# Attention into a feed-forward layer on one core: one third tile's scores in another bank pair, the first q scaled on VectorE and loaded in two pieces, four column sums on quarters of the array, and a longer table of order

## The chip, the cores and the metric

The kernel runs on one core of one Trainium2 chip. The metric is device time in microseconds of one execution, the median over the runs. Before the change three runs gave 1102.1, 1102.84 and 1106.57 us, so the median is 1102.84 us.

## What is computed

The reference takes q, k and v of 8 batches, 8 heads, 576 positions and 64 features, and the weights of a feed-forward layer with 512 inputs, 2048 hidden units and 512 outputs:

```python
scores = scale * np.matmul(q, k.transpose(0, 1, 3, 2))
thresh = np.max(scores, axis=-1, keepdims=True) - tau
scores = np.where(scores >= thresh, scores, -1000000000.0)
attn = np.exp(scores - np.max(scores, axis=-1, keepdims=True))
attn = attn / (np.sum(attn, axis=-1, keepdims=True) + 1e-09)
attn_out = np.matmul(attn, v)
x = attn_out.transpose(0, 2, 1, 3).reshape(B * S, H * D)
h = x @ w_in
g = s * np.maximum(h, 0.0) ** 2 + b
out = g @ w_out
```

The term b of g adds to every output the same row: b times the column sums of w_out. The kernel computes that row once ("the sums") and adds it to each finished block.

## The kernel before

**Tiles.** The scores are made in tiles of 128 rows by 576 keys. Batch 0 is done with float32 products by `plain_tile` (36 tiles of four pairs of heads), batches 1 to 7 with pairs of float16 pieces by `split_tile` (252 tiles). A plain tile goes: two matmuls on TensorE write the scores into a pair of PSUM banks (L531), VectorE takes the row maximum (L534), ScalarE the exponent (L538), VectorE drops what is under the threshold and sums (L540), GpSimd and VectorE make the reciprocal (L543, L545), GpSimd scales the row (L546), TensorE transposes it into bank pair `t` (five transposes, L554), ScalarE copies that out (L558), and TensorE multiplies with v into bank `pv` (L567), which ScalarE copies out (L571). The scores of plain tiles lie in turn in bank pair `s` and, in every second tile, in bank pair `o`.

**Weights.** w_in and w_out arrive in float64 (16 pieces each, L651 and L654, 512 KB a piece), are turned into float32 by two operations on ScalarE (L675, L678) and one on VectorE (L670), their sizes are measured with 16 small matmuls for every four pieces (L693, L697), and when all 32 pieces are known a common power of two is found (L703 to L720). Only then ScalarE (L742) and VectorE (L746) split the weights in float16 halves, and only after that the feed-forward layer can start.

**The sums.** `sums(k)` handles four pieces of w_out: four float32 matmuls with a matrix of ones (L773), two after each other on the left 64 columns of the array and two on the right 64, so that two run side by side. Groups 0 and 1 come in the middle of the weights, groups 2 and 3 later (`SUMS_LATE`). VectorE adds each group to a buffer (L779), and one matmul with the constant `both` (L782) adds the two rows that the halves made.

**Feed-forward.** For a block of 256 rows there are 16 steps of 24 matmuls into bank `h` (in the trace line 280, tile h), a chain on ScalarE and GpSimd (L852, L855, L856, L857), and twice six matmuls into bank pair `o` (line 280, tile o).

**The first q.** `Plain.load` issues a pair's q (two transfers of 64 rows by 576), k and v from SyncE. For every pair GpSimd multiplies q by the scale (`scale_q`, L404), once per head, and the scores wait for that.

**Dummies.** 76 matmuls on constants (L988, `keep_busy`) are put where the plan has TensorE free: 16 at the start and 5 for each of the first twelve tiles. Each one runs, wherever it stands.

**The order.** Nothing is ordered by hand: the class `Plan` holds every piece of work with an engine, a cost, its inputs and a due time, places it by list scheduling forwards and backwards, and prints one fixed order for each engine. The table `NUDGES` moves single runs of operations of one engine and cost (kind, first, how many, by how many ns) before the last placing. Each engine then works strictly in this order and waits where an input is late. All loads leave on one queue, SyncE's.

## Time and profile before

| | us |
|---|---|
| three runs | 1102.1, 1102.84, 1106.57 |
| median | 1102.84 |
| the profiled execution, its own time | 1104.32 |
| its span from the first to the last instruction | 1102.5 |
| what lies around the span | 1.82 |
| TensorE busy | 1087.2 |
| ScalarE busy | 962.2 |
| VectorE busy | 913.0 |
| GpSimd busy | 544.4 |

A busy time is the union of an engine's instructions. Matmuls overlap in the pipeline, and their ends are modelled; so the time that a group of matmuls costs is better read from the chain of waits, where a piece reaches from one start to the next.

### The profile page before, as it was taken

The numbers are of one execution on the slowest core, as the hardware profiler recorded it, in microseconds if no ns is written. First come the engines' busy times: TensorE is split into PE (matmuls) and PEld (weight loads), VectorE is DVE, ScalarE is ACT, GpSimd is POOL, SyncE is SP. The second block draws the span as 40 slices with busy tenths as digits, with TensorE's granted clock in tenths as the row PEclk, the third lists the DMA queues.
The fourth block names the chain that finished last, engine by engine and source line by source line (L and its number), as shares of the span: only waits on it lengthen the run. The fifth ranks groups of instructions, "written<-read, shape, count | busy, mean of one in ns | idle before, by whom it ended". The sixth has DMA issues, their size and how long they took to land.

```text
span 1102.5 us, 38419 instructions
## 1 busy us (share of the span) xinstructions
PE 1087.2 (99%) x15026; PEld 927.5 (84%) x15026; DVE 913.0 (83%) x1947; ACT 962.2 (87%) x2293; POOL 544.4 (49%) x1113
## 2 busy tenths in 40 slices
PE   8999999999999999999999999999999999999998
PEld 7876778888888888788888888888888799997886
DVE  6899899999999899999887999988988888884021
ACT  8998998999899999999889998998999899896443
POOL 6646565555555554555444454444646455443200
PEclk9999999999999999999999999999999999999999
DMA  9940279879968988889876789769976987563000
GB/s 269 360 167 1 68 176 182 153 139 168 211 111 164 197 168 160 149 150 172 156 133 113 145 165 180 137 127 191 169 115 130 161 164 132 99 108 60 2 21 21
DMA packets 359078, 157.05 MB, mean 142 GB/s; under 512 B 313328, under 2 KB 340464, under 8 KB 358896
## 3 DMA queue, kind: packets, MB, share of 16 engines
q1 hardware_dynamic: 358896, 154.60, 70.8%
q8 instruction: 118, 1.93, 0.7%
q14 instruction: 64, 0.52, 0.2%
HBM read 46.01 MB, written 9.44 MB: 50 GB/s over the span
## 4 chain that ended last, share of the span: by engine, by line
PE 89%; DVE 3%; DMA 3%; ACT 2%; issue 1%; SPq 1%; POOL 0%; DVEq 0%; ACTq 0%; POOLq 0%
PE o L280 31%; PE h L280 31%; PE pv L631 8%; PE t L280 5%; PE s L280 5%; PE pv L567 2%; PE t L554 2%; PE o L531 1%; PE s L531 1%; DMA eb<-en 1%; DMA ea<-en 1%; DVE em L607 1%; PE h L693 1%; DVE st L599 1%; PE s L594 1%
## 5 line engine op out<-in xcount | busy, mean ns | idle before, releaser
L280 PE MATMUL h<-xp,iw 128*64 128x256 f16 x6912 | 434.8, 273 | 2.4 <-ACT iw L852 2.2
L280 PEld LDWEIGHTS <-iw 128*64 128x64 f16 x6912 | 393.5, 110 | 31.0 <-issue 5.6
L280 PEld LDWEIGHTS <-gs 128*64 128x64 f16 x3456 | 235.8, 110 | 77.9 <-issue 1.0
L857 POOL TENSOR_TENSOR gs<-iw,gs 128x256 f16<-128x256 f32 x272 | 193.2, 711 | 188.4 <-ACT gs L856 77.8
L280 PE MATMUL o<-ow,gs 128*64 128x512 f16 x1944 | 249.6, 379 | 0.0
L616 DVE SCALAR_TENSOR_TENSOR en<-em,st,en 128x576 f16<-128x576 f32 x252 | 207.3, 826 | 21.2 <-ACT en L613 19.4
L613 ACT ACTIVATE en<-em,st 128x576 f16<-128x576 f32 x252 | 193.1, 770 | 12.1 <-DVE st L612 7.5
L280 PE MATMUL o<-iw,gs 128*64 128x512 f16 x1512 | 196.9, 379 | 0.2 <-DVE iw L876 0.2
L601 POOL TENSOR_SCALAR st<-st,wz 128x1 f32<-128x1 f32 x252 | 130.5, 518 | 101.2 <-DVE st L599 66.4
L852 ACT ACTIVATE iw<-h 128x256 f32<-128x256 f32 x288 | 108.6, 377 | 63.3 <-PE h L280 59.5
L610 POOL TENSOR_SCALAR st<-st 128x1 f32<-128x1 f32 x252 | 87.4, 347 | 148.5 <-DVE em L607 95.8
L855 ACT ACTIVATE iw<-iw 128x256 f32<-128x256 f32 x288 | 119.9, 417 | 3.4
L856 ACT CAST gs<-iw 128x256 f16<-128x256 f32 x288 | 116.1, 405 | 7.2 <-PE o L280 3.9
L280 PEld LDWEIGHTS <-ow 128*64 128x64 f16 x1568 | 100.1, 110 | 18.1 <-issue 2.8
L607 DVE SCALAR_TENSOR_TENSOR em<-s,st,em 128x576 f32<-128x576 f32 x126 | 102.2, 811 | 12.8 <-ACT em L605 8.3
L607 DVE SCALAR_TENSOR_TENSOR em<-t,st,em 128x576 f32<-128x576 f32 x126 | 102.2, 811 | 9.6 <-ACT em L605 5.1
L605 ACT ACTIVATE em<-s,st,wz 128x576 f32<-128x576 f32 x126 | 104.0, 825 | 1.1
L605 ACT ACTIVATE em<-t,st,wz 128x576 f32<-128x576 f32 x126 | 103.7, 823 | 0.8 <-DVE vs L464 0.2
L599 DVE TENSOR_REDUCE st<-s 128x1 f32<-128x576 f32 x126 | 94.3, 749 | 9.2 <-PE s L280 6.9
L599 DVE TENSOR_REDUCE st<-t 128x1 f32<-128x576 f32 x126 | 94.4, 749 | 7.3 <-PE t L280 6.1
L603 ACT ACTIVATE st<-st,wz 128x1 f32<-128x1 f32 x252 | 73.1, 290 | 24.4 <-DVE st L599 23.9
L631 PE MATMUL pv<-eb,ow 128*64 128x256 f16 (+1 forms) x588 | 78.9, 286 | 0.3 <-DMA eb<-en 0.3
(188 smaller groups left out, 1606.8 us busy)
## 6 DMA issues: line engine op xcount, KB each, us to landing
ow<-k SPq DMA_DIRECT2D x98, 216.0 KB, 3.8
rk<-in_k_dram SPq DMA_DIRECT2D x29, 288.0 KB, 3.5
iw<-in_moe_w_in_dram SPq DMA_DIRECT2D x16, 512.0 KB, 9.8
ow<-in_moe_w_out_dram SPq DMA_DIRECT2D x16, 512.0 KB, 9.3
out_dram<-iw SPq DMA_DIRECT2D x32, 256.0 KB, 3.5
rq<-in_q_dram SPq DMA_DIRECT2D x28, 288.0 KB, 4.0
rv<-in_v_dram SPq DMA_DIRECT2D x56, 128.0 KB, 3.2
qs<-k SPq DMA_DIRECT2D x14, 216.0 KB, 4.1
```

Of the source, the lines that this page charges most:

```text
L280: nc.tensor.matmul(out[own], stat[:, own], moving, start=start, stop=stop)
L599: dve((667, 750), lambda: nc.vector.tensor_reduce(out=top, in_=ps, axis=mybir.AxisListType.XY, op=ALU.max, negate=True), [bk], [(ks_, 0)], ...
L601: pool((290, 255), lambda: nc.gpsimd.tensor_scalar(out=line, in0=top, scalar1=-1.0, scalar2=va.wz[:, 2:3], op0=ALU.mult, op1=ALU.add), [(k ...
L605: act((716, 885), lambda: nc.scalar.activation(out=halves, in_=ps, func=AF.Exp, bias=bias, scale=va.wz[:, 1:2]), [bk, (ks_, 4), (va.kwz, 1 ...
L607: dve((738, 820), lambda: nc.vector.scalar_tensor_tensor(out=halves, in0=ps, scalar=line, in1=halves, op0=ALU.is_ge, op1=ALU.mult, accum_o ...
L613: act((666, 760), lambda: nc.scalar.activation(out=pieces[:, 0:S], in_=ex, func=AF.Copy, scale=unit), [em_k, (ks_, 3)], [en_k], i)
L616: dve2((728, 830), lambda: nc.vector.scalar_tensor_tensor(out=pieces[:, S + T:2 * S + T], in0=ex, scalar=unit, in1=pieces[:, 0:S], op0=ALU ...
L631: nc.tensor.matmul(ps[j * D:(j + 1) * D], hd.values()[:, (n + 1) % 5, u * D:(u + 1) * D], lazy[("ea", "eb")[j]][:, n, g.c0:g.c0 + g.n], st ...
L852: act((264, 400), lambda: nc.scalar.activation(out=g(), in_=ps, func=AF.Relu, scale=H_DOWN), [h, (f"w{SPARES[(0, 1, 5)[k3]]}", "i", 2)], [ ...
L855: act((307, 430), lambda: nc.scalar.activation(out=g(), in_=g(), func=AF.Square), [kg], [kg], at)
L856: act((295, 405), lambda: nc.scalar.copy(out=hi, in_=g()), [kg], [f"gh{k3}"], at)
L857: do((735, 735) if not self.last else (400, 490), lambda: eng.tensor_tensor(out=lo, in0=g(), in1=hi, op=ALU.subtract), [kg, f"gh{k3}"], [f ...
```

## The change

- The third tile's scores go to bank pair `t`, which the transposes use, in place of `s`.
- For pair 0 both heads' q are scaled by VectorE; the other pairs stay with GpSimd.
- The first head's q of pair 0 comes in two transfers (columns 0 to 127, and the other 448), each scaled by itself; the first tile waits for the small one alone.
- The four matmuls of a group of sums go to four quarters of 32 columns, side by side, with one row of ones for each quarter in `both` (four memsets in place of two).
- The table `NUDGES` keeps its entries, with the kinds renumbered for the new kinds of operation, and grows from 290 to 706 entries.

```diff
 NUDGES = (
-    (65, 55, 78, 6378), (67, 298, 144, 1003), (67, 501, 22, 5345), (38, 97, 63, -9652), (73, 2, 1, -2466), (53, 128, 6, -1430), (20, 46, 18, 3633), (48, 231, 35, -1881),
+    (68, 55, 78, 6378), (70, 298, 144, 1003), (70, 501, 22, 5345), (41, 97, 63, -9652), (76, 2, 1, -2466), (56, 128, 6, -1430), (23, 46, 18, 3633), (51, 231, 35, -1881),
...
+    (58, 203, 1, 3504), (65, 200, 1, 449), (53, 79, 33, -4132), (67, 65, 15, -2135), (59, 177, 50, 1020), (48, 52, 60, -396), (20, 117, 5, 2817), (8, 0, 4, 162),
...
+    Q = P // 4
...
             for j in range(2):
-                dma(144, lambda j=j: nc.sync.dma_start(out=self.get()[1][j * D:(j + 1) * D, j], in_=qT[self.bi, 2 * self.p + j]),
-                    [], [kq + (j,)], at)
+                cut = ((0, P), (P, S)) if not self.p and not j else ((0, S),)
+
+                def part_(c, j=j):
+                    dma(c[1] / 4, lambda: nc.sync.dma_start(out=self.get()[1][j * D:(j + 1) * D, j, c[0]:c[1]],
+                                                            in_=qT[self.bi, 2 * self.p + j, :, c[0]:c[1]]), [], ["q00" if c[1] == P else kq + (j,)], at)
+                part_(cut[0])
                 if not j:
                     dma(295, lambda: nc.sync.dma_start(out=self.get()[0], in_=kT[self.bi, h2].rearrange("h d s -> (h d) s")),
                         [], [kk], at)
+                if len(cut) > 1:
+                    part_(cut[1])
...
-                pool((740, 748), lambda j=j: self.scale_q(j), [k, (self.tag, "z"), "bound"], [k], at)
+                if not self.p and not j:
+                    dve2((150, 230), lambda: self.scale_q(0, 0, P), ["q00", (self.tag, "z"), "bound"], ["q00"], -40)
+                    dve2((460, 540), lambda: self.scale_q(0, P, S), [k, (self.tag, "z"), "bound"], [k], at)
+                elif not self.p:
+                    dve2((560, 640), lambda j=j: self.scale_q(j), [k, (self.tag, "z"), "bound"], [k], at)
+                else:
+                    pool((740, 748), lambda j=j: self.scale_q(j), [k, (self.tag, "z"), "bound"], [k], at)
...
-        def scale_q(self, j):
-
-            q = self.get()[1][:, j]
-            nc.gpsimd.tensor_scalar(out=q, in0=q, scalar1=scale, scalar2=1.0, op0=ALU.mult, op1=ALU.mult)
+        def scale_q(self, j, lo=0, hi=S):
+
+            q = self.get()[1][:, j, lo:hi]
+            (nc.gpsimd if self.p else nc.vector).tensor_scalar(out=q, in0=q, scalar1=scale, scalar2=1.0, op0=ALU.mult, op1=ALU.mult)
...
             for n, f in enumerate(fs):
-                nc.tensor.matmul(bank["h"][n % 2 * D:(n % 2 + 1) * D], ones.bitcast(F32)[:, 0:D], lazy["whole", f, 1],
-                                 start=(n < 2), stop=(n > 1))
-        plan.add("PE", (2 * 870, 2 * 870 + 250), products, [(f"w{f}", "o") for f in fs] + ["ones"], ["h"], at, True)
+                nc.tensor.matmul(bank["h"][n * Q:(n + 1) * Q], ones.bitcast(F32)[:, 0:Q], lazy["whole", f, 1], start=True, stop=True)
+        plan.add("PE", (870 + 120, 870 + 370), products, [(f"w{f}", "o") for f in fs] + ["ones"], ["h"], at, True)
...
-        for j in range(2):
-            nc.gpsimd.memset(both[j * D:j * D + 1], 1.0)
+        for j in range(4):
+            nc.gpsimd.memset(both[j * Q:j * Q + 1], 1.0)
...
-        ti.tag = "o" if i < TWO_BANKS and i % 2 else "s"
+        ti.tag = "t" if i == 2 else "o" if i < TWO_BANKS and i % 2 else "s"
```

The table's rows tell little, so three places of the resulting order are shown. The first is SyncE's queue at the start of the program, where `rq`, `rk` and `xp` are q, k and v of pair 0, `qs`, `en` and `vt` those of pair 1, `k<-in_q` the q of pair 2, and `iw`, `ow` the weights. Before:

```order
L974 DMA tau_t<-in_tau_dram 128x1
L371 DMA rq<-in_q_dram 64x576
L374 DMA rk<-in_k_dram 128x576
L371 DMA rq<-in_q_dram 64x576
L395 DMA xp_129<-in_v_dram 128x2x256
L371 DMA qs<-in_q_dram 64x576
L374 DMA en_77<-in_k_dram 128x576
L395 DMA vt<-in_v_dram 128x2x256
L371 DMA qs<-in_q_dram 64x576
L651 DMA iw_195<-in_moe_w_in_dram 128x4x256
```

With the change:

```order
L1038 DMA tau_t<-in_tau_dram 128x1
L431 DMA rk<-in_k_dram 128x576
L427 DMA qs<-in_q_dram 64x576
L460 DMA xp_131<-in_v_dram 128x2x256
L427 DMA k<-in_q_dram 64x576
L427 DMA rq<-in_q_dram 64x128
L427 DMA qs<-in_q_dram 64x576
L427 DMA rq<-in_q_dram 64x576
L427 DMA rq<-in_q_dram 64x448
L460 DMA vt<-in_v_dram 128x2x256
L431 DMA en_77<-in_k_dram 128x576
L716 DMA iw_200<-in_moe_w_in_dram 128x4x256
```

The first q, the first transfer behind tau before, now stands behind k of pair 0, a q of pair 1, v of pair 0 and a q of pair 2; the first weights move from the tenth to the twelfth place.

The second place is TensorE at the start (`s`, `o`, `t` are the bank pairs, `em` the exponents of a tile, `pv<-qt,ones` the dummies). Before:

```order
L988 MATMUL pv<-qt,ones 128x256 x16
L531 MATMUL s<-rk,rq 128x288 x2
L531 MATMUL o<-rk,rq 128x288 x2
L988 MATMUL pv<-qt,ones 128x256 x10
L531 MATMUL s<-rk,rq 128x288 x2
L531 MATMUL o<-rk,rq 128x288 x2
L988 MATMUL pv<-qt,ones 128x256 x2
L554 MATMUL t<-eb,em_78 128x128 x5
L988 MATMUL pv<-qt,ones 128x256 x8
L554 MATMUL t<-eb,em_79 128x128 x5
L531 MATMUL s<-en_77,qs 128x288 x2
```

With the change:

```order
L1052 MATMUL pv<-qt,ones 128x256 x16
L596 MATMUL s<-rk,rq 128x288 x2
L1052 MATMUL pv<-qt,ones 128x256 x5
L596 MATMUL o<-rk,rq 128x288 x2
L1052 MATMUL pv<-qt,ones 128x256 x5
L596 MATMUL s<-en_77,qs 128x288 x2
L619 MATMUL t<-eb,em_78 128x128 x5
L596 MATMUL o<-rk,rq 128x288 x2
L619 MATMUL t<-eb,em_79 128x128 x5
L596 MATMUL t<-rk,rq 128x288 x2
```

The same 16 dummies stand ahead of the first scores; a tile of pair 1 now comes third, and the tile whose scores lie in `t` comes fifth.

The third place is VectorE at the start. Before:

```order
L1002 TENSOR_SCALAR bound<-bound 128x1
L534 TENSOR_REDUCE st_69<-s 128x1
L534 TENSOR_REDUCE st_70<-o 128x1
L540 SCALAR_TENSOR_TENSOR em_78,st_69<-s,st_69,em_78 128x576
L540 SCALAR_TENSOR_TENSOR em_79,st_70<-o,st_70,em_79 128x576
```

With the change:

```order
L1066 TENSOR_SCALAR bound<-bound 128x1
L469 TENSOR_SCALAR rq<-rq,bound 128x128
L599 TENSOR_REDUCE st_69<-s 128x1
L469 TENSOR_SCALAR rq<-rq,bound 128x576
L469 TENSOR_SCALAR rq<-rq,bound 128x448
L605 SCALAR_TENSOR_TENSOR em_78,st_69<-s,st_69,em_78 128x576
L599 TENSOR_REDUCE st_70<-o 128x1
```

The three scalings now stand in VectorE's queue, the last of them (the 448 columns) ahead of the first tile's own threshold step.

Further on, the order of all engines differs in most places by a few positions. Ahead of the first feed-forward matmul TensorE's order holds 135 transposes (L554) and 140 products with v (L567) before, and 130 and 130 with the change; scores, sizes, sums and dummies are the same in number. Up to ScalarE's last weight conversion (L678) its order holds 24 exponents, 21 copies and 10 evacuations before, and 22, 19 and 9 with the change. Between matmuls on the whole array, on halves and on quarters TensorE changes 53 times before and 51 times with the change.

## Rows read from the trace of the kernel before

**Rows 1.** The page's first part: busy time by engine.

```profile
PE 1087.2 (99%) x15026; PEld 927.5 (84%) x15026; DVE 913.0 (83%) x1947; ACT 962.2 (87%) x2293; POOL 544.4 (49%) x1113
```

**Rows 2.** Busy time by stretch: PE, PEld, DVE, ACT, POOL; PEclk, DMA share, GB/s.

```profile
5.00:10.00 5.00, 4.79 (x20) 3.53 (x18) 1.64 (x3) 3.00 (x6) 2.14 (x5) 1.00 1.00 244
10.00:20.00 10.00, 8.43 (x61) 6.90 (x61) 8.53 (x20) 7.59 (x14) 6.57 (x15) 1.00 1.07 331
20.00:60.00 40.00, 40.00 (x360) 31.73 (x357) 35.73 (x77) 39.70 (x73) 24.86 (x44) 1.00 1.07 350
60.00:92.20 32.20, 31.85 (x309) 23.14 (x308) 31.22 (x74) 27.52 (x50) 17.24 (x40) 1.00 0.27 88
92.20:96.30 4.10, 4.07 (x36) 3.00 (x34) 4.10 (x8) 4.10 (x8) 3.08 (x5) 1.00 0.00 0
96.30:135.00 38.70, 38.55 (x465) 29.22 (x466) 35.06 (x69) 36.16 (x77) 25.43 (x36) 1.00 0.19 49
135.00:1098.20 963.20, 956.05 (x13774) 826.47 (x13770) 793.74 (x1695) 839.94 (x2066) 461.46 (x942) 1.00 0.74 138
```

**Rows 3.** TensorE's waits, whole run: waited for, us, times, longest.

```profile
PE s L280 <- DVE em L607: 2.9, 3, 2.0
PE h L280 <- ACT iw L852: 2.2, 5, 0.6
...
PE s L531 <- DVE em L540: 1.0, 1, 1.0
```

**Rows 4.** Timeline, 0 to 13 us: start us, us, engine, line; idle before.

```profile
1.18 0.59 SPq L371 DMA_DIRECT2D rq<-in_q_dram  x1
...
1.51 3.79 PE L988 MATMUL pv<-qt,ones 128*128 128x256 f32 x16 [1.51 <-POOL qt L978]
...
3.59 0.48 SPq L371 DMA_DIRECT2D qs<-in_q_dram  x1
...
4.47 0.75 POOL L404 TENSOR_SCALAR rq<-rq,bound 128x576 f32<-128x576 f32 x1
...
5.30 2.27 PE L531 MATMUL s<-rk,rq 128*128 128x288 f32 x4
...
8.84 0.75 POOL L404 TENSOR_SCALAR qs<-qs,bound 128x576 f32<-128x576 f32 x1 [2.27 <-DMA qs<-in_q_dram]
...
10.75 1.24 PE L531 MATMUL s<-rk,rq 128*128 128x288 f32 x4 [0.96 <-DVE em L540]
...
12.59 0.67 ACT L675 ACTIVATE iw<-iw 128x512 f32<-128x512 f32 x1 [2.41 <-DMA iw<-in_moe_w_in_dram]
```

**Rows 5.** DMA table, 0 to 8 us: transfer, count, KB, us to landing.

```profile
rq<-in_q_dram SPq DMA_DIRECT2D x2, 144.0 KB, 3.2
...
xp<-in_v_dram SPq DMA_DIRECT2D x1, 256.0 KB, 4.9
```

**Rows 6.** Chain of waits, 0 to 100 us: start, us, what.

```profile
24.07 0.55 PE t L554 x5
24.61 1.24 PE pv L567 x20
...
26.52 0.97 PE s L531 x4
...
32.20 1.17 PE s L531 x4
...
37.83 1.72 PE h L773 x8
```

**Rows 7.** Timeline of VectorE: the first weight split; a wait near 880 us.

```profile
92.24 0.86 DVE L746 SCALAR_TENSOR_TENSOR iw<-iw,wpower 128x512 f16<-128x512 f32 x1
...
878.52 0.76 DVE L456 TENSOR_REDUCE vm<-rk 128x1 bf16<-128x576 f32 x1 [3.11 <-DMA rk<-in_k_dram]
```

**Rows 8.** Timeline of TensorE: the first feed-forward matmuls; a wait near 880 us.

```profile
96.35 1.50 PE L280 MATMUL h<-xp,iw 128*64 128x256 f16 x24
...
880.72 0.68 PE L280 MATMUL s<-qs 128*64 128x288 f16 x8 [1.96 <-DVE em L607]
```

More of the change, by code (lines that the diff above doesn't have):

```diff
@@ L919, in make_tiles @@
                     ti.st = lambda i=i, j=j: [(fl, A.get()[1][:, j, us[0] * NB + i * P:us[0] * NB + (i + 1) * P], A.get()[0])]
-                    ti.kq = lambda j=j: [A.keys[0], A.keys[1] + (j,), (A.tag, "z")] + A.kept[0]
+                    ti.kq = lambda j=j, i=i: [A.keys[0], A.keys[1] + (j,) if i or j or pair or us[0] else "q00", (A.tag, "z")] + A.kept[0]
                     ti.slot, ti.plain = j, j and (A, [(0, fl), (1, fl)], xb[xk][:, pair, i * P:(i + 1) * P],
```

121 rows, old and new, of the table NUDGES are left out of this document.

## The prediction

> **What bounds the kernel now.** I read four views, in this order. The page's first part shows TensorE busy for 1087.2 us, ScalarE for 962.2, VectorE for 913.0 [rows 1]. So the end is TensorE's: the time is the work in its queue plus the time that it stands idle, and a change counts by what it does to these two. The stretches show where it stands idle [rows 2]: 0.21 and 1.57 us between 5 and 20 us, nothing from 20 to 60, 0.35 to 92.2, next to nothing around the start of the feed-forward layer, and 7.15 us in the 963.2 us from 135 to 1098.2. With the 1.51 us ahead of its first matmul [rows 4] and the 4.3 us behind its last one (1102.5 less 1098.2) that is 15 us in all. The waits name what stood behind them [rows 3]: a threshold step of VectorE (2.9 us, three times), the evacuation of `h` on ScalarE (2.2 us, five times), and in the start one wait of 1.0 us for the first tile's threshold step. The granted clock is 1.00 in every stretch, so the clock plays no part.
>
> The busy start is less full than it looks: the 76 dummies stand in it. They run in both kernels, 16 of them ahead of the first scores, so TensorE's time there is fixed by its order and by when the first operands come.
>
> VectorE is busy for 31.22 of the 32.2 us before the weights are split, ScalarE for 39.70 of 40 from 20 to 60 us [rows 2]. The first feed-forward matmul at 96.35 us [rows 8] comes four microseconds after VectorE's first weight split at 92.24 [rows 7]. TensorE is full until there, but VectorE is nearly so as well.
>
> **The sums, part by part.** A group of sums is 8 rows in the trace (each float32 matmul runs in two passes) and takes 1.72 us of the chain [rows 6]: two matmuls after each other on each half, so 0.86 us for one pair side by side. Four quarters side by side need one such stretch: 0.86 us saved, four times, **-3.4 us** of TensorE's work. No row shows quarters. The bounds come from the halves: if quarters overlap only in twos, nothing is saved; if not at all, four stretches of 0.86 make 3.44 in place of 1.72, 6.9 us lost in all. I take the full saving, since the halves do run beside each other and the quarters read the same rows and write separate partitions.
>
> A change between arrangements of the array has a price in the rows: scores behind work on the whole array take 0.97 us to the next piece, behind the halves of L567 1.17 [rows 6], so 0.20. The orders show 53 changes before and 51 with the change, so **-0.4 us** at most, and I take it; the bound on the other side is 0. The Trainium skill says in TensorEngine Tiling (Array Packing), section Tiling Modes, that changing the mode (not just the tile) drains the engine, which speaks against a third mode; the 0.20 us agree with it. By that rule the quarters pay at each of their own entries and exits, all of which are in the 51, so the sum would be the same.
>
> **The first q.** Before, it leaves at 1.18 us as the first transfer behind tau, GpSimd has it by 4.47, and the scores start at 5.30, the moment at which the 16 dummies end (1.51 plus 3.79) [rows 4]. Now 288, 144, 256 and 144 KB stand ahead of it, 832 KB together. The same number stood ahead of the first `qs` before (144, 288, 144, 256), issued at 3.59, for which GpSimd waited until 8.84 [rows 4]. The new piece is 112 KB smaller than that `qs`; at the 244 GB/s of the stretch [rows 2] that is 0.5 us, so it lands at about 8.4. The ends: 3.2 us from issue to landing, as the first q had [rows 5], gives 6.8; as late as `qs`, 8.8. The scaling of 128 columns lies between a small step and the 0.75 us of the 576 columns on GpSimd [rows 4]; I take 0.25, and 0.1 for the handover. The first scores then start at 8.7 in place of 5.3: **+3.4 us** of idle TensorE (+1.9 to +3.9), and nothing covers it, since the dummies behind stand behind in the order too.
>
> The scaling moves from GpSimd to VectorE: three steps of together 0.5 to 1.5 us. VectorE has 3.4 of 5 us free there [rows 2], so this costs nothing by itself. The Trainium skill gives in VectorE: DVE Perf Modes, section The perf-mode tier table, twice the element rate for a tensor_scalar on float32 in SBUF; by that I estimate 1.1 us for the three, which would change nothing in the sum. But the last of them waits for the 448 columns, the ninth transfer, and the first tile's threshold step stands behind it.
>
> **The third tile.** Before, the third scores waited 0.96 us for the first tile's threshold step to free `s` [rows 4], and the waits of the start come to 1.8 us in all (0.21 plus 1.57). With `t` the third tile is free of that, but the order puts a tile of pair 1 in `s` in its place, behind the same step, and the `t` tile two transposes later. I take the same 1.8 us, **0**, with 0 to 4 us as bounds (-1.8 to +2.2).
>
> **What moves.** Ahead of the feed-forward layer TensorE's order holds five transposes and ten products fewer (20 rows of the trace), 0.55 and 1.24 us [rows 6]. They come later, so TensorE's work is the same. The first weights leave behind 144 KB more (1808 in place of 1664), 0.4 us at 331 GB/s [rows 2], and were waited for until 12.59 [rows 4]; ScalarE has two exponents, two copies and one evacuation fewer up to its last conversion, over 2 us, so it is not later there. The extra transfer costs SyncE half a microsecond as any issue does (0.48 and 0.59) [rows 4], and two more memsets lie on GpSimd where it waits for `qs`. **0**.
>
> **The rest of the order.** It is different almost everywhere, and no row says how much of the 7.15 us of idle time stays. I take it as unchanged, with 0 and twice as much as ends (-7.15 to +7.15). The largest wait shows its kind: 1.96 us of TensorE near 880 us [rows 8], behind a size step of VectorE that waited 3.11 us for its k [rows 7]. Such waits come from how long ahead a load stands, and in both orders the loads stand two to five tiles ahead.
>
> **The sum.** -3.4 - 0.4 + 3.4 + 0 + 0 + 0 is -0.4 us, to be set against the profiled execution's own 1104.32 us: 1103.9. That execution is 1.48 us above the median of the runs shown (1102.84), so the forecast is **1102.4 us**, no change. A measurement of this kernel can tell about 0.5% from no change, 5.5 us, so faster begins under 1097.3 and slower above 1108.4.
>
> **The rivals.** *A smoother order*: the many new entries of the table take away between half and all of the 7.15 us: 1102.4 less 3.6 to 7.15, so 1095.3 to 1098.8. For it: the waits are few and each has one late input. Against: 0.7% idle is little to take from, and a new order has late inputs of its own.
>
> *VectorE holds the feed-forward layer.* TensorE's queue ahead of it is shorter by 3.4 and 1.8 us, but VectorE's is not: it gains the three scalings and its first threshold step is later by over a microsecond. If its first weight split does not come before 92.24, the first feed-forward matmul stays at 96.35 or comes up to 2.5 us later, the saving turns into idle time, and the 1.8 us behind are left over: 1104.6 to 1107.1, slower than before. It decides from the point at which that split starts later than 90.0 (92.24 less what TensorE can gain there, 5.2 and 0.4 less 3.4). For it: 31.22 of 32.2 us busy. Against: VectorE is idle for 4.3 us between 20 and 60 us [rows 2], which a different order can use.
>
> *The quarters don't run side by side*: the change doesn't do what it says. In twos 1105.8, one by one 1112.7.
>
> *A rougher order*: idle time doubles behind the start, 1109.6.
>
> *The first q comes early after all* (6.8 us): 1100.9, inside the forecast's own spread.
>
> **How the numbers follow.** Forecast with the bounds of the start and of the changes of arrangement (1099.1 to 1105.5) 0.49, smoother order 0.24, VectorE 0.15, quarters 0.06 (0.02 of it one by one), rougher order 0.06. Three quarters of the smoother case, with the start's lower bounds beside it, lie under 1097.3: faster 0.18. Slower takes the rougher order, the quarters one by one and 0.02 of the VectorE case: 0.10. The same has 0.72. The range leaves out the best of the smoother order and the slower cases: 1095.5 to 1107.5.
>
> **What would show it.** In the changed profile: sums of 0.9 us in the chain (right) or 1.7 (wrong); the first scores at 8 to 9 us; no row of `t` waiting for VectorE at the third tile; the first feed-forward matmul at 94 to 95 us; idle time from 135 us on near 7 us. The prediction is wrong if the first scores start before 7 us, if the first feed-forward matmul comes before 92 or after 97, or if idle time behind 135 us is under 3 or over 11 us.

## The result, and the profile after

The changed kernel takes **1114.91 us** (median of 4 runs, 1113.81 to 1116.04), the kernel before 1103.78 beside it (1102.1 to 1106.57): a ratio of **1.0105, with an interval of 1.0091 to 1.0118**. It is slower by some 11 us, or 1%. The forecast was 1102.4 with a range up to 1107.5; it was wrong, and the time lies outside the range.

The profiled execution has a span of 1111.9 us, 9.4 more than before's. In this kernel's numbering the scores are L596 (before: L531), the row maximum L599, the transposes L619, the sums L838, the first weight split on VectorE L811, the feed-forward products L333. The page's first part:

```profile
PE 1088.3 (98%) x15026; PEld 940.6 (85%) x15026; DVE 915.2 (82%) x1950; ACT 959.1 (86%) x2293; POOL 545.2 (49%) x1113
```

Busy times have hardly moved against [rows 1] (TensorE +1.1 us, VectorE +2.2, ScalarE -3.1). The 9 us are time in which the engines wait for one another. The same stretches as in [rows 2], then 60 us up to the first feed-forward matmul, and everything ahead of it (columns as there):

```profile
5.00:10.00 5.00, 2.00 (x7) 1.28 (x5) 0.72 (x1) 1.69 (x4) 2.23 (x3) 1.00 1.05 277
10.00:20.00 10.00, 7.96 (x34) 5.48 (x32) 6.86 (x15) 5.87 (x10) 3.84 (x8) 1.00 1.05 363
20.00:60.00 40.00, 38.50 (x351) 31.17 (x352) 34.21 (x74) 38.31 (x70) 23.33 (x40) 1.00 1.07 358
60.00:101.45 41.45, 38.56 (x368) 27.44 (x367) 39.38 (x94) 35.40 (x64) 22.14 (x51) 1.00 0.17 49
0.00:101.45 101.45, 90.51 (x769) 68.86 (x770) 82.77 (x188) 85.48 (x151) 55.00 (x134) 1.00 0.67 217
```

The same row of the kernel before, up to its first feed-forward matmul:

```profile
0.00:96.35 96.35, 92.62 (x792) 71.79 (x792) 82.85 (x184) 86.16 (x153) 57.47 (x135) 1.00 0.72 228
```

This pair of rows is the main reading. VectorE does the same work ahead of the feed-forward layer, 82.85 and 82.77 us, but stands idle for 18.7 us in place of 13.5: 5.2 us more, and the layer starts 5.1 us later. TensorE does 2.1 us *less* there and stands idle for 10.9 us in place of 3.7, ScalarE for 16.0 in place of 10.2. So no engine got more work; which one the others wait for, this pair of rows does not say.

The timeline of the opening and of the layer's start (start us, us, engine, line; in brackets the idle time before and who ended it):

```profile
7.51 0.72 DVE L469 TENSOR_SCALAR rq<-rq,bound 128x128 f32<-128x128 f32 x1 [3.34 <-DMA rq<-in_q_dram]
...
8.29 2.29 PE L596 MATMUL s<-rk,rq 128*128 128x288 f32 x4 [3.00 <-DVE rq L469]
...
11.29 0.89 DVE L469 TENSOR_SCALAR rq<-rq,bound 128x576 f32<-128x576 f32 x2
...
11.86 1.98 PE L596 MATMUL o<-rk,rq 128*128 128x288 f32 x4 [0.21 <-DVE rq L469]
...
14.66 0.74 ACT L603 ACTIVATE em<-o,st 128x576 f32<-128x576 f32 x1 [2.51 <-DVE st L599]
15.30 0.66 ACT L740 ACTIVATE iw<-iw 128x512 f32<-128x512 f32 x1
...
37.29 1.07 PE L838 MATMUL h<-ow,ones 128*32 128x512 f32 x8
...
97.28 0.75 DVE L811 SCALAR_TENSOR_TENSOR iw<-iw,wpower 128x512 f16<-128x512 f32 x1
...
101.45 1.17 PE L333 MATMUL h<-xp,iw 128*64 128x256 f16 x18
```

The first scores come 3.0 us late, the second tile's at 11.86 (behind the scaling of the second head's q, which before was done by 6.6), ScalarE's first weight step at 15.30 in place of 12.59, the first weight split at 97.28 in place of 92.24. TensorE's longest waits, whole run:

```profile
PE h L333 <- ACT iw L916: 3.2, 7, 0.7
PE s L596 <- DVE rq L469: 3.0, 1, 3.0
PE o L596 <- DVE em L605: 1.7, 3, 0.7
...
PE t L596 <- ACT en L623: 1.0, 1, 1.0
```

The last one is the third tile: it no longer waits for VectorE but for ScalarE, which has to copy the second tile out of the shared bank `t` first.

From the first feed-forward matmul to the end of the span it takes 1010.45 us (before 1006.15), 4.3 more. Of these 1.8 are the five transposes and ten products that were moved behind it, as forecast. So the account of this pair of profiles, 9.4 us in all, is **5.1 us ahead of the layer, 1.8 moved behind it, and 2.5 behind it that no row names**. The last figure is weak: from the first feed-forward matmul to the end, profiles of kernels that have one order there take from 1003.7 us (merged, below) over 1006.15 (before) to 1011.45 (old_order).

### The profile page after: what moved, and what is told of

It is laid out like the page before. It is cut to its first block, busy times and chain, and to the rows that moved or that the text cites. A ratio compares the mean times of both kernels' runs of the same rounds, so it can differ in the third digit from the quotient of the medians.

```text
span 1111.9 us, 38386 instructions
## 1 busy us (share of the span) xinstructions
PE 1088.3 (98%) x15026; PEld 940.6 (85%) x15026; DVE 915.2 (82%) x1950; ACT 959.1 (86%) x2293; POOL 545.2 (49%) x1113
## 4 chain that ended last, share of the span: by engine, by line
PE 64%; ACT 8%; DVE 5%; DMA 4%; issue 3%; SPq 0%; POOL 0%; DVEq 0%; ACTq 0%
PE h L333 24%; PE o L333 24%; PE pv L696 7%; PE t L333 3%; PE s L333 3%; ACT en L678 2%; ACT em L670 2%; DMA eb<-en 2%; DMA ea<-en 1%; DMA rv<-in_v_dram 1%; DVE em L672 1%; DVE en L681 1%; DVE st L664 1%; ACT iw L916 1%; DVE vm L521 1%
## 5 line engine op out<-in xcount | busy, mean ns | idle before, releaser
L333 PE MATMUL h<-xp,iw 128*64 128x256 f16 x6912 | 435.9, 273 | 3.5 <-ACT iw L916 3.2
L333 PEld LDWEIGHTS <-iw 128*64 128x64 f16 x6912 | 395.4, 110 | 33.5 <-issue 9.2
L333 PEld LDWEIGHTS <-gs 128*64 128x64 f16 x3456 | 246.8, 110 | 69.3 <-issue 1.0
L921 POOL TENSOR_TENSOR gs<-iw,gs 128x256 f16<-128x256 f32 x272 | 197.3, 726 | 182.7 <-ACT gs L920 82.8
L333 PE MATMUL o<-ow,gs 128*64 128x512 f16 x1944 | 250.5, 379 | 0.0
L678 ACT ACTIVATE en<-em,st 128x576 f16<-128x576 f32 x252 | 193.0, 770 | 18.3 <-DVE st L677 8.8
L333 PE MATMUL o<-iw,gs 128*64 128x512 f16 x1512 | 197.4, 379 | 0.4 <-DVE iw L940 0.2
L666 POOL TENSOR_SCALAR st<-st,wz 128x1 f32<-128x1 f32 x252 | 133.8, 531 | 107.5 <-DVE st L664 67.1
L333 PEld LDWEIGHTS <-ow 128*64 128x64 f16 x1568 | 101.8, 110 | 16.3 <-issue 2.6
```

The lines of the kernel that those rows point to most:

```text
L333: nc.tensor.matmul(out[own], stat[:, own], moving, start=start, stop=stop)
L666: pool((290, 255), lambda: nc.gpsimd.tensor_scalar(out=line, in0=top, scalar1=-1.0, scalar2=va.wz[:, 2:3], op0=ALU.mult, op1=ALU.add), [(k ...
L678: act((666, 760), lambda: nc.scalar.activation(out=pieces[:, 0:S], in_=ex, func=AF.Copy, scale=unit), [em_k, (ks_, 3)], [en_k], i)
L921: do((735, 735) if not self.last else (400, 490), lambda: eng.tensor_tensor(out=lo, in0=g(), in1=hi, op=ALU.subtract), [kg, f"gh{k3}"], [f ...
```

## The experiments

Three theories at the start. *First q*: what is lost is the late first q, about 3 us. *Order*: the planner's new order, which follows from new costs and from the table `NUDGES`, fits worse, and the parts are harmless. *Parts*: the bank, the scalings or the quarters themselves cost. "First FFN" is the start of the first feed-forward matmul in the profile (before 96.35, the change 101.45). It stands for one execution and repeats to about 1 us: where two kernels have the same instructions in the same order up to some point, they still stand up to 1.0 us apart there, and that difference arises in the first 30 us (merged and relieved 0.66 us at 86 us, the change and new_to_ffn 1.0). Each ratio is to the kernel before as it ran beside that run; its medians were 1103.76 to 1104.42 us. In the code cuts, lines in words stand for longer code.

| run | us, median | ratio to before, 95% | first FFN |
|---|---|---|---|
| the change | 1114.91 | 1.0091 to 1.0118 | 101.45 |
| q_first | 1111.99 | 1.0049 to 1.0093 | 98.86 |
| q_late_alone | 1107.0 | 1.0013 to 1.0041 | 98.69 |
| quarters_alone | 1103.93 | 0.9982 to 1.0005 | 96.42 |
| table_290 | 1123.04 | 1.014 to 1.0195 | 105.23 |
| cost_only | 1121.06 | 1.0143 to 1.017 | 102.03 |
| old_order | 1105.74 | 1.0008 to 1.0037 | 96.35 |
| head_old | 1116.99 | 1.0094 to 1.0132 | 103.03 |
| head_new | 1112.3 | 1.0064 to 1.0101 | 104.40 |
| old_to_ffn | 1110.5 | 1.0049 to 1.0076 | 96.57 |
| new_to_ffn | 1112.47 | 1.006 to 1.0086 | 102.74 |
| old_order_t | 1112.59 | 1.0063 to 1.0107 | 101.05 |
| no_bank_t | 1123.24 | 1.0159 to 1.0189 | 101.86 |
| undo_pool | 1114.56 | 1.008 to 1.0109 | 101.37 |
| fill | 1113.25 | 1.0073 to 1.0099 | 99.47 |
| halves_in_change | 1114.56 | 1.0083 to 1.0112 | 104.54 |
| merged | 1102.66 | **0.9975 to 0.9995** | 95.56 |
| more_dve | 1107.33 | 1.0017 to 1.0047 | 96.93 |
| relieved | 1104.72 | 0.9999 to 1.0017 | 96.22 |

### The late first q: q_first, q_late_alone

q_first, the change with pair 0's loads at the head of the queue:

```diff
     work = plan.run()
+    ahead = [tau, q00, k, q of head 1, rest of q of head 0]      # loads of pair 0
+    work = ahead + [n for n in work if n not in ahead]
```

> The changed kernel with the three transfers of pair 0's q and its k moved to the head of the load queue; nothing else moves. If the place of the first q is what costs (theory 1), the first scores start near 5.5 us in place of 8.3, the 3.0 us wait goes, the first feed-forward matmul comes 3 to 5 us earlier than 101.4 and the time falls from 1114.9 to 1110 to 1112. If the rest of the new order holds VectorE back (theory 2), the first scores come early all the same, but the first feed-forward matmul stays at 100 to 102 us and the time within 1.5 us of 1114.9.

q_late_alone, the same edit in the kernel before, with its loads in the change's order (tau, k, first `qs`, v, a q of pair 2, then the first q whole):

> The kernel before with only the opening loads in the order of the changed kernel (pair 0's q in sixth and eighth place, whole, still scaled by GpSimd). Theory 1: the first scores at about 9 us, 3 to 4 us of TensorE idle, the first feed-forward matmul 3 to 5 us later and the time up by 3 to 5 us to 1107 to 1109. Theory 2: the stretch between 20 and 92 us takes the delay up, time up by less than 1.5 us.

Both say the same: taking the late q away gives 2.6 us back at the first FFN and 2.9 us in the end, putting it in alone costs 2.3, less than the 3 to 5 expected, and some 3 us in the end. In q_late_alone the delay is whole by 18 us (VectorE's row maxima 2.35 us behind before's) and the same at 86 us: what is lost in the opening is carried on, neither caught up nor made worse. The theory holds for a quarter of the loss, and for no more: with the first q early the change is still 0.5 to 0.9% slow.

### The order or the parts: cost_only, table_290, old_order

cost_only is the kernel before with one figure of its planner changed, and with not one instruction more, fewer or other:

```diff
-        plan.add("PE", (2 * 870, 2 * 870 + 250), products, ...
+        plan.add("PE", (870 + 120, 870 + 370), products, ...
```

> The kernel before with nothing edited but the figure by which its planner costs the sums (990 instead of 1740 ns for four instructions); the sums stay on halves and the instructions are the same, only their order follows the new plan. Theory O (the table of nudges fits one plan, and any replanning loses by its order alone): 1107 to 1120 us. Theory P (the loss comes from this change's own parts, the bank and the opening): 1102 to 1105 us.

It loses 17 us, more than the change. All that is ahead of its first feed-forward matmul, and the FFN stretch behind:

```profile
0.00:102.05 102.05, 95.22 (x804) 73.93 (x805) 82.69 (x190) 87.57 (x156) 59.57 (x142) 0.98 0.66 215
```
```profile
135.00:1098.00 963.00, 949.58 (x13609) 810.01 (x13609) 800.39 (x1692) 834.23 (x2055) 460.25 (x944) 1.00 0.73 138
```

VectorE's work is once more 82.7 us, its idle time 19.4. TensorE is idle for 13.4 us behind 135 us, where before has 7.15 [rows 2]. table_290 is the change with the 416 new entries of the table left out (`NUDGES[:290]`):

> The changed kernel with only the first 290 entries of the table, so the four changes of structure stay and the 416 new entries go. Theory 2 (the new entries make an order that VectorE and ScalarE follow badly) expects the time to come back to 1100 to 1106. Theory 1 has the first q third in the queue here, so it expects the start without the wait of 3 us and 1108 to 1112 with whatever else the structure costs.

It loses 19 us, where one theory expected 1100 to 1106 and the other 1108 to 1112. So the old table fits the old plan, and both new plans that were run with it lose 17 to 19 us; the new entries won 7 to 8 of these back, not all. The opposite test, old_order, emits the changed kernel's operations in a written-down copy of the order of before (third tile in `s`):

```diff
-        return [ops[n][3] for _, n in self.order]
+        return [ops[n][3] for n in ORDER]      # the order of before, new operations beside the old ones
...
-        ps = bank[bk]                          # plain_tile
+        ps = bank["s" if bk == "t" else bk]
```

> The changed kernel's operations (first heads' q in two transfers and scaled by VectorE, sums on quarters) in the order of the kernel before, written down as a fixed list; the third tile stays in the bank that it had before, since the bank of the transposes is not free for it at that place in this order. Theory 1 (the loss lies in the new order and in the late first q; the operations themselves cost nothing): 1102 to 1105 us. Theory 2 (the scalings on VectorE, 0.72 + 0.89 us in the trace of the change, push VectorE's later work): 1105 to 1107 us, the first weight split behind 93.5 us. If it comes out at 1110 us or more, the operations carry the loss and the order is innocent.

The first FFN is back at 96.35, scalings on VectorE, two transfers and quarters included, though the first scores start 1.2 us late (6.46, behind k of pair 0); by 18 us all but 0.2 us of that is made good. These parts cost nothing ahead of the layer in this order. What is left, about 2 us (0.08 to 0.37%), arises behind it; why stays open.

quarters_alone puts only the sums on quarters, in the order of before:

```diff
-                nc.tensor.matmul(bank["h"][n % 2 * D:(n % 2 + 1) * D], ones.bitcast(F32)[:, 0:D], lazy["whole", f, 1],
-                                 start=(n < 2), stop=(n > 1))
+                nc.tensor.matmul(bank["h"][n * 32:(n + 1) * 32], ones.bitcast(F32)[:, 0:32], lazy["whole", f, 1], start=True, stop=True)
```

> The kernel before, in its own order, with only the sums on quarters. If TensorE bounds the stretch ahead of the feed-forward layer, the 2.9 us that the four groups get shorter (1.00 in place of 1.72 us each) come off: 1100.9. If VectorE holds it (the rival of the prediction), the first feed-forward matmul stays at 96.3 us and the time within 1 us of 1103.8.

No gain. A group of sums does take 1.07 us in the rows in place of 1.72 [rows 6], 1.00 to the start of the next piece, so TensorE's work gets 2.9 us shorter; the first FFN stays where it was.

### Where in the order: old_to_ffn, new_to_ffn, head_old, head_new

Mixed orders, cut at a point of the plan: all operations planned ahead of it in one kernel's order, the rest in the other's (changed operations in all four; the third tile's bank follows the first part).

```diff
+    first = [n for n in one_order if start_in_its_plan(n) < cut]      # cut: the first FFN product, or 20 us
+    ORDER = first + [n for n in other_order if n not in first]
```

> The changed kernel's operations in the order of before up to the first FFN product (third tile in its old bank, loads in the order of before), and in the change's own order from there on. If the new order loses on both sides of that point: first FFN matmul at 96 to 97 us as in before, and 1106 to 1110 us, the change's own losses behind the FFN's start being left. If all that counts lies ahead of the FFN: 1103 to 1105.5 us.

> The mirror: the change's own order up to the first FFN product, the order of before from there on. Both sides lose: first FFN matmul at 101 to 102 us and 1107 to 1111 us. All ahead of the FFN: 1112 to 1116 us.

Both sides lose: behind the layer's start the change's order costs about 0.4% (old_to_ffn over old_order, whose parts it shares: 1.0063 less 1.0022, 4.5 us, and the intervals lie apart), more than the 2.5 us of the pair of profiles. Ahead of it the change's order costs 8 us with the late q and the moved 1.8 us in it; here 1112.47 lies in the range that was given for "all ahead of the FFN", so this mirror alone does not decide. The two don't add up to the 11.1 us exactly. A cut at 20 us tells less:

> The changed kernel with the kernel before's order for the work of the first 20 us (loads included, so the first q comes early; third tile in its old bank) and the change's own order for all that is left. Theory A (the loss arises in the opening, from the first q, the second head's q and the third tile, and is only carried on): 1102 to 1105 us. Theory B (the new order loses throughout): the opening's share alone is won back, 2.5 to 4 us, which gives 1109.5 to 1112.5 us.

> The mirror of the run before: the changed kernel with its own order for the work of the first 20 us (late first q, third tile in the bank of the transposes) and the kernel before's order for the rest. Theory A (all of the loss is in the opening): 1112 to 1116 us. Theory B (the new order loses throughout): 1106.5 to 1109 us, that is the opening's 2.5 to 4 us over the kernel before.

head_old was expected to win back at least the opening and won nothing (1.0094 to 1.0132, the change 1.0091 to 1.0118). Its seam explains that: TensorE stands for 4.71 us at the place where the orders meet.

```profile
28.15 1.30 PE L860 MATMUL t<-eb,em 128*128 128x128 f32 x5 [4.71 <-ACT x L864]
```

So a mix says something only where its seam is looked at. head_new, the mirror, starts the layer later than the change itself (104.40), though all but 20 us of its order are the old one. Its 1112.3 us fit theory A, but near its seam TensorE waits too (1.78 us at 26.45), so it proves no more than head_old.

### The third tile's bank: old_order_t, no_bank_t

old_order_t is old_order with the bank as the change has it, and the least reordering that this asks for (the third tile's scores behind the first two tiles' copies, and what depends on them behind that):

```diff
-        ps = bank["s" if bk == "t" else bk]
+        ps = bank[bk]
+    ORDER: each operation as early as the order of before has it, but behind all that it depends on
```

> As old_order, but the third tile's scores go to the bank of the transposes, as in the change, and stand behind the first two tiles' transposes; the order of all else is the kernel before's as far as this allows. Theory T (the bank holds the third tile, and with it the stretch ahead of the FFN): the third tile's scores start some 3 to 5 us later than in old_order, and the whole is 2 to 4 us above it, 1107.5 to 1110 us. Theory O (only the planned order loses, the bank is harmless): 1104.5 to 1107 us.

Here a part does cost. The ten microseconds from 10 us, old_order first, then old_order_t:

```profile
10.00:20.00 10.00, 9.44 (x68) 7.71 (x68) 8.92 (x21) 8.39 (x15) 6.80 (x14) 1.00 1.07 344
```
```profile
10.00:20.00 10.00, 8.02 (x45) 6.21 (x45) 5.50 (x12) 5.63 (x10) 3.76 (x8) 1.00 1.05 329
```

VectorE falls from 8.92 us of work to 5.50, and the first FFN comes 4.7 us later; the time, 1112.59, is above what either theory expected. TensorE's timeline of old_order_t shows how (L837 scores, L860 transposes):

```profile
17.45 1.24 PE L837 MATMUL t<-rk,rq 128*128 128x288 f32 x4
...
22.99 0.76 PE L860 MATMUL t<-eb,em 128*128 128x128 f32 x5 [2.15 <-POOL em L852]
```

The third tile can start only when the first two are transposed and copied out, at 17.45 in place of 11.71, and it holds `t` until its threshold step has read it. So nothing is transposed until its own transposes come at 22.99, for which TensorE waits 2.15 us; in old_order there are two more groups of transposes by then, at 18.46 and 22.00. Two users that had a bank each now take turns in one. In the change's own plan the bank can't be taken away by itself, since the plan shifts with it:

```diff
-        ti.tag = "t" if i == 2 else "o" if i < TWO_BANKS and i % 2 else "s"
+        ti.tag = "o" if i < TWO_BANKS and i % 2 else "s"
```

> The changed kernel, planned anew with its own table of nudges, with the third tile in its old bank. Theory T: the stretch ahead of the FFN gets 2 to 3 us shorter, 1111 to 1113 us. Theory O: the table fitted the plan with the bank, so that taking the bank away is one more disturbance, 1114 to 1124 us.

That run loses 19 us, as theory O expected (first FFN 101.86, the rest behind it). With the plan shifted as well, it says nothing on the bank.

### The scalings and TensorE's slow opening: undo_pool, fill

undo_pool lets GpSimd scale pair 0's q in the change's order:

```diff
-            (nc.gpsimd if self.p else nc.vector).tensor_scalar(out=q, ...)
+            nc.gpsimd.tensor_scalar(out=q, ...)
```

> The changed kernel in its own order, with the three scalings of the first heads' q done by GpSimd again (0.75 us for a whole row of 576 in the trace of before). If VectorE's two scalings ahead of its first threshold step (0.89 us together) hold the opening, this gives back about 1 us: 1113 to 1114.5 us. If the second head's scores, which wait for their scaling, hold it, GpSimd, which is idle there, gives back the same or up to 2 us. If the scaling by VectorE was right and quicker, it is slower, 1115 to 1116.5 us.

No difference that can be told (1114.56). Which engine scales is not what matters. fill puts 12 more dummies ahead of the first scores:

```diff
+        def idle_(m):
+            for _ in range(m): nc.tensor.matmul(bank["pv"][:, P:P + NB], ones, qt[:, 0:NB], start=True, stop=True)
...
+            lambda m=13 if not r and i == n - 1 else 1: idle_(m)      # the last of the 16 makes 13
```

> The changed kernel in its own order with 12 more of the idle-time products (28 instead of 16) ahead of the first scores, which fill TensorE's 3.0 us of waiting there. In the trace of the change the first scores took 0.69 to 0.85 us each and the idle-time products 0.336 us until 13.4 us, in the trace of before 0.41 and 0.16 us from 7.4 us on. If TensorE's pace there hangs on having been idle, the second tile's scores come 0.5 to 1.5 us earlier and the time is 1113 to 1114.5 us; if the pace in the opening has another cause, or VectorE holds the second tile anyway, no difference: 1114.5 to 1116 us.

```profile
8.12 1.24 PE L596 MATMUL s<-rk,rq 128*128 128x288 f32 x4 [1.21 <-DVE rq L469]
...
10.63 1.24 PE L596 MATMUL o<-rk,rq 128*128 128x288 f32 x4 [0.68 <-DVE rq L469]
```

With 12 more dummies ahead of them, the first scores take 1.24 us in place of 2.29 and the second tile's start 1.2 us earlier; the first FFN gains 2.0 us, all of it there by 14 us. The median is 1.7 us under the change's, but the two intervals overlap, so the gain in the end is likely rather than shown.

### What paces the stretch: halves_in_change, merged, more_dve, relieved

Theory V: VectorE paces everything ahead of the feed-forward layer, so TensorE's savings are worth nothing. halves_in_change takes the quarters out of the change, in the change's order:

```diff
-                nc.tensor.matmul(bank["h"][n * Q:(n + 1) * Q], ones.bitcast(F32)[:, 0:Q], lazy["whole", f, 1], start=True, stop=True)
+                nc.tensor.matmul(bank["h"][n % 2 * D:(n % 2 + 1) * D], ones.bitcast(F32)[:, 0:D], lazy["whole", f, 1],
+                                 start=(n < 2), stop=(n > 1))
```

> The changed kernel in its own order with the sums on halves again (1.72 instead of 1.07 us for a step of eight records). Theory V (VectorE paces): the 2.9 us that TensorE saves by the quarters are worth nothing, 1114 to 1115.8 us. Rival (they are worth their time in the change's order): 1116.5 to 1118 us.

```profile
0.00:104.55 104.55, 93.80 (x770) 70.40 (x770) 82.37 (x188) 85.85 (x151) 54.96 (x132) 1.00 0.65 210
```

A miss for the theory as it stood: ahead of the layer the quarters *are* worth 3.1 us in the change's order. It is not the chance of one execution: VectorE's row maxima run 0.15 us ahead of the change's at 36 us and then 0.9, 1.5, 2.2 and 3.1 us behind them, one step for each group of sums.

```profile
35.88 0.76 DVE L599 TENSOR_REDUCE st<-s 128x1 f32<-128x576 f32 x1
...
101.84 0.74 DVE L599 TENSOR_REDUCE st<-s 128x1 f32<-128x576 f32 x1
```

The same two in the change:

```profile
36.03 0.74 DVE L599 TENSOR_REDUCE st<-s 128x1 f32<-128x576 f32 x1
...
98.75 0.74 DVE L599 TENSOR_REDUCE st<-s 128x1 f32<-128x576 f32 x1
```

So in the change's order TensorE's work counts there, and VectorE alone does not set the layer's start. In the end nothing of the 3.1 us is seen (1114.56 against 1114.91); where they go behind the layer's start stays open.

merged lets TensorE add the fourth group of sums onto the third in the bank and drops one of VectorE's additions; more_dve doubles all three; relieved is merged with two reductions moved to later:

```diff
 merged
-      start=True, stop=True)                        # sums on quarters
+      start=(k < 3), stop=(k != 2))
...
-      dve(..., lambda: nc.vector.tensor_tensor(out=part, in0=bank["h"], in1=part, op=ALU.add), ...)
+      dve(..., lambda: k == 2 or nc.vector.tensor_tensor(out=part, in0=bank["h"], in1=part, op=ALU.add), ...)
 more_dve (sums on halves)
+      nc.vector.tensor_tensor(out=part, in0=part, in1=part, op=ALU.max)      # behind each addition
 relieved, on top of merged
+    late = the two row maxima of raw k and q of the second group (L456)
+    work = work without late; late put in ahead of the third of their kind
```

> The kernel before in its own order, sums on quarters; the third block's sums stay in the bank and the fourth block's are added to them there by TensorE, so that one of VectorE's three additions ahead of the FFN (0.68 us in the trace of before) falls away. Theory V (VectorE paces the stretch ahead of the FFN): the first FFN matmul comes 0.6 to 1.2 us earlier, at 94.9 to 95.5 us by the clock on which before's is at 96.1, and the time is 1101.5 to 1103.3 us. Rival (TensorE or ScalarE paces it): the first FFN matmul stays within 0.2 us.

> The kernel before in its own order, sums on halves, with one more VectorE instruction behind each of the three additions (the greater of the running sums and themselves, 128x512, which changes nothing): about 3 x 0.6 = 1.8 us more of VectorE ahead of the first weight split. Theory V: first FFN matmul 1.5 to 2.2 us later, 97.6 to 98.3 us, time 1105 to 1106.5 us. Rival: within 0.3 us of before.

> As merged, and two of VectorE's reductions over the second group's raw k and q (0.73 + 0.74 us at 90.3 us in the trace of before), whose results are wanted at 131 us only, are moved behind the first splits, right ahead of the third of their kind at 128 us. Theory V: 2.1 us less of VectorE ahead of the first weight split, so the first FFN matmul at 93.9 to 94.7 us and the time 1100.5 to 1103 us, under both kernels. Rival (another engine takes over the bound after the first 0.7 us): 95 to 95.5 us and a time like merged's.

merged gains 0.79 us at the first FFN, as expected, and about 1.1 in the end. relieved brings VectorE's first split to 90.85, but its layer starts only 0.13 us earlier than before's and 0.66 later than merged's; more_dve costs 0.58 us where three additions of 0.7 were put in. These differences are no larger than what single executions differ by, so they are better read from an instruction that all of them run shortly before, with the same work ahead of it in merged and relieved. In merged and in relieved:

```profile
86.33 1.26 DVE L832 SCALAR_TENSOR_TENSOR xp<-x,power,xp 128x1024 f16<-128x1024 f32 x1
```
```profile
86.99 1.26 DVE L832 SCALAR_TENSOR_TENSOR xp<-x,power,xp 128x1024 f16<-128x1024 f32 x1
```

From its start to the first FFN it takes 9.76 us in the kernel before, 9.56 in quarters_alone, 9.23 in merged, 9.23 in relieved and 10.59 in more_dve. So the dropped addition is worth 0.3 us there, the two reductions moved to later nothing, and the additions put in behind this point cost 0.8: another engine takes over, as relieved's rival had it. Its time is not like merged's, though: 1104.72 us, and the intervals lie apart, so moving the reductions costs some 2 us behind the layer's start. more_dve ends 3.5 us above before, again mostly behind that start. Why another engine takes over stands in ScalarE's timeline of the kernel before:

```profile
90.11 1.33 ACT L742 ACTIVATE iw<-iw,wpower 128x512 f16<-128x512 f32 x2
...
95.62 0.67 ACT L783 ACTIVATE gs<-h,b_t 128x512 f32<-128x512 f32 x1
96.19 0.73 ACT L538 ACTIVATE em<-o,st 128x576 f32<-128x576 f32 x1
```

and in that of relieved (VectorE, ScalarE, TensorE):

```profile
90.85 0.74 DVE L746 SCALAR_TENSOR_TENSOR iw<-iw,wpower 128x512 f16<-128x512 f32 x1
...
95.48 0.69 ACT L782 ACTIVATE gs<-h,b_t 128x512 f32<-128x512 f32 x1
...
96.22 1.17 PE L280 MATMUL h<-xp,iw 128*64 128x256 f16 x18 [0.37 <-ACT gs L782]
```

The first feed-forward matmul waits for ScalarE to read the last sum out of `h` (L783; L782 in merged and relieved), and ScalarE is busy without a break from the moment the weights' common power of two is known, at 90.1 us. Up to that moment VectorE's work counts: the addition that merged drops lies ahead of it, at 88.04 in the trace of before, and one of more_dve's extra ones at 88.49. Behind it ScalarE counts, and what VectorE saves there is worth nothing. In the order of before theory V thus agrees with what was tried ahead of 90 us, and fails beyond; in the change's order it fails ahead of 90 us too (halves_in_change). There the layer's first matmul does not wait for that read either: TensorE comes to it without a break from scores at 100.28 that had waited 0.56 us for VectorE.

## Why the prediction was wrong, point by point

- **The rest of the order (taken as 0, bounds 7.15 us either way).** This is the step that failed. "It is different almost everywhere, and no row says how much ... I take it as unchanged" gave the new order the same fit as the old. cost_only shows what a new plan costs with a table made for another: 17 us, over twice the bound, with the same instructions. In the change itself the parts without bank and order cost 0.2% (old_order), so some 9 of the 11 us lie in order, late q and bank together; the late q has some 3 of them, and the other 6 are order and bank. The bound was taken from TensorE's idle time behind 135 us, as if nothing could be lost ahead of the layer.
- **The third tile (0).** Also failed. The wait for VectorE went, as forecast, but the account stopped at the wait's length. In the order of before the bank, with the little reordering that it forces, costs 4.7 us at the first FFN, since VectorE stands idle until the bank is free and the transposes take turns with it. In the change's own plan its share can't be split from the order's.
- **The first q (+3.4).** Right. First scores at 8.29 where 8.7 was forecast, and 2.9 us back when it is undone. The piece landed earlier (scaled from 7.51), while the scaling took 0.72 us, not 0.25.
- **The sums (-3.4).** Right as to TensorE: 1.00 us a group in place of 1.72, so -2.9, since a stretch with four quarters takes 1.00 and not 0.86. Wrong as to the time: nothing in the order of before, 3.1 us at the first FFN but nothing in the end in the change's. So 3.4 of the 11.5 us between the forecast's -0.4 and the measured +11.1 are this saving; with it at 0 the forecast would have been 1105.8, still inside the range. What failed here is to take TensorE's idle time as it was when its work shrinks. That quarters run side by side agrees with what the Trainium skill says in TensorEngine Tiling (Array Packing), section Tiling Modes: different tiles work in parallel.
- **What moves (0).** The 1.8 us of tile work behind the layer came as forecast. "ScalarE ... is not later there" was wrong: its first weight step came at 15.30, 2.7 us late, because the second tile's exponent stands ahead of it and waited 2.51 us for VectorE.
- **The rivals.** "VectorE holds the feed-forward layer" named the direction and a deciding point (a first split later than 90.0; it came at 97.28), with a chance of 0.15 and a price up to 1107.1. Its mechanism, a saving of TensorE that turns into idle time, fits the order of before (quarters_alone) but not the change's (halves_in_change), so that its sign came true is in part luck. The price was short, since it took VectorE's idle time as fixed and added only the three scalings. That idle time grew by 5.2 us. "A rougher order" gave 1109.6 from idle time behind the start that doubles; it did not double (8.0 us for 7.15), and the larger loss lay ahead. The nearest figure, 1112.7, is that of quarters one by one, which did not happen. By the forecast's own signs, the first feed-forward matmul behind 97 us said that it was wrong; the idle time behind 135 us did not.
- **The clock.** "The clock plays no part" was read from the granted clock alone. [rows 4] already held four rows of scores that took 2.27 us at 5.30 and 1.24 at 10.75, and fill, where the first scores are quick, won 2.0 us at the first FFN.

What stays open: how the loss behind the layer's start arises (4.5 us by old_to_ffn), and the 2 us of old_order there; and how the 6 us of order and bank divide.

**A version that beats both** came out of it: merged, 1102.66 us, a ratio to before of 0.9985 (0.9975 to 0.9995). It is a small gain, and it keeps the order of before. Whether the quarters or the dropped addition make it is not shown: its interval overlaps that of quarters_alone (0.9982 to 1.0005).

## What to carry to other kernels

Where an order is made by a planner and tuned by a table of corrections, a change of one cost is a change of the whole order: try each part in the old order, written down, before planning anew, and price a new plan by a run with only the cost changed. Where several engines are nearly full ahead of a point that all wait for, add up each engine's busy and idle time up to that point; a saving on one engine counts only as far as another doesn't wait for something else, and the engine that counts can change on the way and with the order. Before a difference of under 1 us is read from two profiles, look whether they already differ at an earlier instruction that both share. A bank that is shared by two kinds of user costs the turns that they take, not only the wait that it spares.

## What was not expected of the hardware

In the opening TensorE's float32 matmuls ran at about half the pace for a while. The first scores took 2.29 us in the change, behind 3.0 us of idle time, and 1.24 in fill, behind 28 dummies and 1.21 us of idle time. The idle time alone doesn't decide it: the same four rows took 2.27 us in the kernel before, right behind the 16 dummies [rows 4], 2.26 in old_order behind 1.17 us of idle time, and 1.24 in quarters_alone, whose order is that of the kernel before. How long the slow pace lasts differs too: before, the scores at 10.75 took 1.24 us, while in the change those at 11.86 still took 1.98. The granted clock of that stretch reads 1.00 in the change's rows, the higher of the two levels, but 0.81 in q_late_alone, where the same scores took the same 2.29 us:

```profile
5.00:10.00 5.00, 1.75 (x5) 1.18 (x4) 0.00 (x0) 1.70 (x4) 1.09 (x2) 0.81 1.01 276
```

So like durations stand beside both readings of the column, and the durations of like matmuls are the safer sign. The Trainium skill, TensorE: Matmul & The Clock Gate, section Seeing it yourself, warns that the trace's clock events are unreliable, and these rows agree. A late operand can thus cost twice, once the wait and then slow matmuls behind it: with the q as late as in the change, fill still won 2.0 us at the first FFN.

The scaling of 128 columns on VectorE took 0.72 us in the record, while the two of 448 and 576 columns took 0.89 together. The first one's record begins as the transfer lands and may hold some waiting: in q_first and old_order, where the operand had landed before, the same 128 columns took 0.34 and 0.35 us.
